# Small hashed shifts of the due times in a list-scheduled attention and two-layer feed-forward kernel

## The chip, the cores and the metric

The kernel runs on one NeuronCore of one Trainium2 chip. The metric is the time of one execution on the device, in microseconds (us): 919.58 is the median of three runs of the kernel before (918.4, 919.58, 921.48).

## What is computed

Windowed causal attention, then two feed-forward layers on its output, all in float32 with an error that a single low-precision pass doesn't reach:

```python
scores = q @ k.T / sqrt(64) + alibi bias            # 4 batches, 8 heads, 576 positions, window 128
attn = exp(scores - max) / (sum + 1e-9)
x = (attn @ v)                                      # 2304 tokens x 512
g = x @ w_gate; x = (g * sigmoid(g)) * (x @ w_val) @ w_out1     # inner width 1536
h = x @ w_in;   out = (h * sigmoid(h)) @ w_out2                 # inner width 2048
```

## The kernel before, in words

The 2304 tokens are 18 tiles of 128, worked through in three parts of six tiles. Each part runs the first layer (`moe1`) and the second (`moe2`); the attention of the next part runs between their products. Every float32 operand is split into a high and a low half (`copy_op` or L353 makes the high one, `sum_op` or L362/L363 the low one), and each product is three matmuls: high by high, high by low, low by high (`passes`, L932 to L934; `out1`, L1296 to L1298; `late_out2`, L1217 to L1219; `out2`, L1329 to L1331). The wide products go by a Strassen-like scheme (`quad`): seven products instead of eight on sums of operands and weights, in three PSUM banks X, Y and Z. Between them ACT copies a bank to SBUF (`copy` in `quad`, L353 into `tmp`) and DVE adds a copy to a bank (L979, L994). `operands` (L713, L353, L362) makes the sums and halves of the inputs at the start of each layer. Attention has its own lines: transposes L450 and L458, scores L498, masks L525, bias and maximum L532, exponent L538, the inverse of the row sum L554 and L555, scaling L558 on POOL, a transpose L575, a copy to `u` (L353), two triangular selections L582 and L589, the product with v L612 and its halves L353 and L653. Weights are loaded (L771), turned into words (L772 on ACT into `top`, L775 on DVE into `word`), split, kept in DRAM and fetched again by the parts that follow (L792, L921).

No order of work is written out. Each piece is given to `Plan.add` with an engine, a cost in ns, a due time in ns and the keys that it reads and writes. `Plan.issue` then plays the engines against the clock of its costs: again and again it takes, over all engines, the piece that can start first; where several on an engine are ready, the one with the earliest due time goes first (`insort(ready[e], (ops[n][1], n))`). Pieces that can run on two engines (`copy_op`: ACT or DVE; `sum_op`: POOL or DVE) go to the one that is expected to end sooner. What comes out is one fixed instruction order for each engine and for SP's queue of DMAs; on the chip every engine takes its instructions in that order and waits where an input isn't there yet. So a due time decides two things only: who goes first among the ready, and with it which engine a piece lands on.

Of the kernel before, what the change touches and what calls it, by code (L numbers as in the profile page):

```python
# [20 lines left out]
P = 128  # L21
BIG = 1.0e9
HUGE = 3.0e38


COST = {
# [30 lines left out]
class Plan:  # L57
# [19 lines left out]
    def add(self, engine, cost, due, fn, reads=(), writes=(), take=None, give=None, port=False, other=(), slack=0.0):  # L77
        n = len(self.ops)
        preds = set()
        for key in reads:  # L80
            if key in self.writer:
                preds.add(self.writer[key])
            self.readers.setdefault(key, []).append(n)
        for key in writes:
            if key in self.writer:
                preds.add(self.writer[key])
            preds.update(self.readers.pop(key, ()))
            self.writer[key] = n
        preds.discard(n)
        if isinstance(take, Bank):  # L90
            take = (take,)
        ways = {e: (c, f, p or e == "pool", d) for e, c, f, p, d in [(engine, cost, fn, port, 0.0), *other]}
        self.ops.append((ways, due, preds, take, give, slack))

    def issue(self):
        ops = self.ops
# [107 lines left out]
def attention_moe_moe2_kernel(  # L204
# [303 lines left out]
    def attend(i, hf, dues, banks):  # L508
# [7 lines left out]
        def scores(e, due):  # L516
# [12 lines left out]
            def biased():  # L529
                for p in range(2):  # L530
                    l = 2 * p + e
                    nc.vector.tensor_tensor_reduce(  # L532
                        t[:, l, :], cur()[:, p, :], alibi[:, 4 * hf + l, :], 1.0, HUGE, ALU.add, ALU.min, st[:, 0, l:l + 1]
                    )
# [272 lines left out]
    def strassen_sums(a, due, slack=0.0):  # L807
        def add(x, y, op):
            i = take("sum", len(SUM_R))
            t, tk = SUM_R[i], ("sum", i)  # L810
            (xa, xk), (ya, yk) = x, y
            sum_op(2 * P, due, lambda: t, lambda: xa, lambda: ya, op, xk + yk, [tk], slack=slack)
            return t, [tk]

        s1 = add(a[1, 0], a[1, 1], ALU.add)
        s2 = add(s1, a[0, 0], ALU.subtract)
        s3 = add(a[0, 0], a[1, 0], ALU.subtract)
        s4 = add(a[0, 1], s2, ALU.subtract)
        return s1, s2, s3, s4
# [732 lines left out]
```

## Time and profile before

| | |
|---|---|
| median of three runs | 919.58 us (918.4 to 921.48) |
| the profiled execution | 919.92 us; its span, first to last instruction, 918.2 us |
| TensorE matmul (PE) busy | 899.8 us, 98% of the span, 5938 matmuls |
| VectorE (DVE) busy | 724.0 us, 79% |
| GpSimd (POOL) busy | 605.5 us, 66% |
| ScalarE (ACT) busy | 556.5 us, 61% |
| chain that ended last | PE 76%, DVE 12%, ACT 4%, POOL 4%, DMA 3%, issue 2% |

Busy PE is not PE at its peak: matmuls are pipelined, the end of each is modelled, and two in a row overlap. A wait therefore shows smaller as idle time than it costs. The distance between the starts of two matmuls is the honest measure.

### The profile page before, as it was taken

The page shows a single profiled execution, that of the slowest core. Times are in us where ns is not written, and L with a number is a line of the kernel's source. Part 1 is how long each engine was busy: PE and PEld are TensorE (multiplying, and loading weights), DVE is VectorE, ACT ScalarE, POOL GpSimd, SP SyncE. Part 2 cuts the span into 40 slices and gives each one's busy share as a digit, 9 for nine tenths or more (in the row PEclk, how much of TensorE's full clock was granted, in tenths as well). Part 3 has the DMA queues.
Part 4 walks back from the last instruction along what each step waited for, and adds up shares of the span by engine and source line. Part 5 has one row for each costly group of instructions (what it writes and reads, how often), then busy time and mean ns, then how long its engine had stood idle before and what let it go on. Part 6 is the DMA issues. An engine that isn't in the chain of part 4 may idle for free.

```text
span 918.2 us, 18574 instructions
## 1 busy us (share of the span) xinstructions
PE 899.8 (98%) x5938; PEld 850.3 (93%) x5938; DVE 724.0 (79%) x1687; ACT 556.5 (61%) x1431; POOL 605.5 (66%) x697
## 2 busy tenths in 40 slices
PE   8999999999999999999999999999999999999998
PEld 7888999999888888999999899999799999999997
DVE  8898978989899898879888989897736666836664
ACT  6877666767867775865555586664463333484531
POOL 3756657875767588996566787686444446697564
PEclk9999999999999999999999999999999999999999
DMA  9998878896687977998878577679788788578702
GB/s 224 283 290 253 288 260 289 285 301 218 227 278 239 290 267 260 316 335 277 267 237 287 160 255 266 226 266 342 269 270 254 250 249 252 184 247 251 233 1 92
DMA packets 179233, 230.34 MB, mean 251 GB/s; under 512 B 68160, under 2 KB 90432, under 8 KB 179136
## 3 DMA queue, kind: packets, MB, share of 16 engines
q1 hardware_dynamic: 179136, 229.17, 77.7%
q8 instruction: 47, 0.77, 0.4%
q14 instruction: 50, 0.41, 0.1%
HBM read 152.31 MB, written 76.81 MB: 250 GB/s over the span
## 4 chain that ended last, share of the span: by engine, by line
PE 76%; DVE 12%; ACT 4%; POOL 4%; DMA 3%; issue 2%; SPq 0%; DVEq 0%; POOLq 0%; ACTq 0%
PE bank L932 16%; PE bank L933 15%; PE bank L934 15%; PE bank L612 3%; PE bank L1217 3%; PE bank L1219 3%; PE bank L1218 3%; PE bank L1329 3%; PE bank L498 3%; PE bank L1331 3%; PE bank L1330 3%; PE bank L1296 2%; PE bank L1297 2%; PE bank L1298 2%; POOL ACC L363 2%
## 5 line engine op out<-in xcount | busy, mean ns | idle before, releaser
L932 PE MATMUL bank<-XOP,wu 128*128 128x384 f32 (+1 forms) x868 | 297.2, 342 | 6.7 <-ACT tmp L353 4.9
L933 PE MATMUL bank<-XOP,wu 128*128 128x384 f32 (+1 forms) x868 | 288.8, 333 | 2.1 <-DVE XOP L362 1.3
L934 PE MATMUL bank<-XOP,wu 128*128 128x384 f32 (+1 forms) x868 | 288.6, 332 | 0.0
L932 PEld LDWEIGHTS bank<-XOP,wu 128*128 128x128 f32 x868 | 163.0, 188 | 18.0 <-ACT tmp L353 9.5
L933 PEld LDWEIGHTS bank<-XOP,wu 128*128 128x128 f32 x868 | 163.3, 188 | 3.6 <-DVE XOP L362 2.1
L934 PEld LDWEIGHTS bank<-XOP,wu 128*128 128x128 f32 x868 | 163.0, 188 | 0.0
L353 ACT ACTIVATE tmp<-bank 128x384 f32<-128x384 f32 x139 | 65.1, 489 | 60.5 <-PE bank L934 38.5
L363 POOL TENSOR_TENSOR h<-tmp,h 128x384 fp32r<-128x384 f32 x67 | 68.3, 1028 | 36.9 <-ACT h L353 36.4
L1194 DVE TENSOR_TENSOR ACC<-bank,ACC 128x384 f32<-128x384 f32 (+2 forms) x144 | 74.4, 551 | 3.9 <-PE bank L934 1.6
L363 POOL TENSOR_TENSOR wu<-word,wu 128x256 fp32r<-128x256 f32 x60 | 51.5, 864 | 34.9 <-ACT wu L353 14.5
L558 POOL TENSOR_TENSOR cs<-cs,st 128x512 f32<-128x512 f32 x36 | 39.4, 1093 | 51.3 <-DVE st L555 17.1
L979 DVE TENSOR_TENSOR bank<-bank,tmp 128x384 f32<-128x384 f32 x93 | 51.9, 559 | 21.0 <-PE bank L934 16.1
L772 ACT ACTIVATE top<-raw 128x512 f16<-128x512 bf16 x68 | 54.2, 797 | 20.7 <-DVE word L775 16.3
L1194 DVE TENSOR_TENSOR XST<-bank,XST 128x512 f32<-128x512 f32 (+1 forms) x108 | 57.3, 553 | 11.8 <-PE bank L1219 6.0
L363 POOL TENSOR_TENSOR wu<-sums,wu 128x256 fp32r<-128x256 f32 x79 | 63.1, 824 | 4.3 <-ACT wu L353 2.3
L775 DVE SCALAR_TENSOR_TENSOR word<-raw,top 128x512 int32<-128x512 int32 x68 | 56.6, 833 | 7.2 <-ACT top L772 6.3
L353 ACT ACTIVATE h<-tmp 128x384 fp32r<-128x384 f32 x75 | 38.9, 522 | 37.0 <-DVE tmp L1067 12.3
L538 ACT ACTIVATE cs<-cs,st 128x128 f32<-128x128 f32 x144 | 56.1, 394 | 7.9 <-DVE st L532 7.7
L1329 PE MATMUL bank<-wo,h 128*128 128x512 f32 (+1 forms) x146 | 58.5, 401 | 0.3 <-DVE XOP L362 0.3
L363 POOL TENSOR_TENSOR wo<-word,wo 128x256 fp32r<-128x256 f32 (+1 forms) x34 | 32.8, 967 | 39.2 <-ACT wo L353 31.9
L1331 PE MATMUL bank<-wo,h 128*128 128x512 f32 (+1 forms) x146 | 57.4, 393 | 0.0
L1330 PE MATMUL bank<-wo,h 128*128 128x512 f32 (+1 forms) x146 | 57.4, 393 | 0.0
(400 smaller groups left out, 2478.3 us busy)
## 6 DMA issues: line engine op xcount, KB each, us to landing
wu<-kept_i SPq DMA_DIRECT2D x112, 256.0 KB, 3.1
wu<-kept_g SPq DMA_DIRECT2D x72, 256.0 KB, 3.5
wu<-kept_v SPq DMA_DIRECT2D x72, 256.0 KB, 3.2
kept_s<-wo SPq DMA_DIRECT2D x66, 256.0 KB, 2.7
raw<-in_moe_w_out_dram SPq DMA_DIRECT2D x28, 512.0 KB, 5.3
kept_i<-wu SPq DMA_DIRECT2D x56, 256.0 KB, 4.6
kept_g<-wu SPq DMA_DIRECT2D x42, 256.0 KB, 5.3
kept_v<-wu SPq DMA_DIRECT2D x42, 256.0 KB, 5.4
```

What stands on the lines that cost most here:

```text
L353: act = lambda: nc.scalar.activation(out(), src(), AF.Copy)
L363: pool = lambda: nc.gpsimd.tensor_tensor(out(), x(), y(), op)
L538: nc.scalar.activation(t[:, l, :], t[:, l, :], AF.Exp, bias=st[:, 0, l:l + 1], scale=-1.0, accum_out=st[:, 1, l:l + 1])
L772: plan.add("act", 650.0, due, lambda: nc.scalar.activation(top16, bits, AF.Copy), [rk], [tk])
L775: lambda: nc.vector.scalar_tensor_tensor(w.bitcast(I32), word, 13, top, ALU.logical_shift_right, ALU.bitwise_or),
L932: nc.tensor.matmul(ps, wh, xh, start=start, stop=False, skip_group_check=True)
L933: nc.tensor.matmul(ps, wh, xl, start=False, stop=False, skip_group_check=True)
L934: nc.tensor.matmul(ps, wl, xh, start=False, stop=stop, skip_group_check=True)
L1194: plan.add("dve", cost("dve", n), due, lambda: nc.vector.tensor_tensor(acc, pv(), acc, ALU.add), [b], keys, give=b)
L1329: nc.tensor.matmul(ps, hh, wh, start=(i == 0), stop=False)
L1330: nc.tensor.matmul(ps, hh, wl, start=False, stop=False)
L1331: nc.tensor.matmul(ps, hl, wh, start=False, stop=(i == 1))
```

## The change

Each due time under `BIG` gets a shift that depends on the number of the piece and on a seed; the seed is looked up in a table by the 10 us stretch of planned time that the due time lies in. Seed 0 leaves the stretch alone. 34 of the 88 stretches have another seed: the shift then lies between -599 and +599 ns. 2532 of the 5759 pieces get one. The ten blank lines after `handover` make room, so that every line after it stands 13 lower in the new file.

```diff
+ORDER = (
+    1, 0, 0, 7, 2, 6, 0, 0, 0, 0, 8, 0, 0, 0, 0, 12, 0, 0, 0, 0, 0, 0, 0, 0, 0, 0, 10, 0, 15, 5, 0, 0, 0,
...
+)
+
+
+def shifted(due, n):
+
+    w = int(max(due, 0.0) // 10000)
+    seed = ORDER[w] if w < len(ORDER) else 0
+    return due + (((n + 1) * (2 * seed + 1) * 40503 >> 3) % 1024 - 511.5) * 1.1719 if seed and due < BIG else due
...
-        self.ops.append((ways, due, preds, take, give, slack))
+        self.ops.append((ways, shifted(due, n), preds, take, give, slack))
```

Over the whole program no instruction is added or removed, but some change engine: 26 pieces go from DVE to POOL, 17 from POOL to DVE, 22 from ACT to DVE and 16 from DVE to ACT. On PE 1396 of 1638 pieces keep their order among themselves, on SP's queue 681 of 804 (and no transfer moves more than nine places). Three places show what it does.

ACT at the start of the program, around the copy of the transposed weights of the second head half to `u` (`u_124`), which L612 on PE multiplies with v. Before:

```order
L538 ACTIVATE cs,st_121<-cs,st_121 128x128 x2
L353 ACTIVATE wu_73<-word_95 128x256
L461 ACTIVATE qts<-bank_130 128x256
L353 ACTIVATE wu_74<-word_95 128x256
L772 ACTIVATE top_94<-raw_92 128x512
L353 ACTIVATE u_124<-bank_131 128x512
L538 ACTIVATE cs,st_122<-cs,st_122 128x128 x2
```

With the change:

```order
L474 ACTIVATE qts<-bank_132 128x256
L785 ACTIVATE top_94<-raw_91 128x512
L366 ACTIVATE KR<-bank_129 128x2x128
L366 ACTIVATE u_124<-bank_135 128x512
L366 ACTIVATE u_123<-bank_130 128x512
L474 ACTIVATE qts<-bank_131 128x256
```

The copy to `u_124` has moved up past two weight halves (`wu`) and the conversion of a second weight tile (`top_94<-raw_92`).

DVE at 505 to 511 us, around the low halves of two hidden blocks (`h_105`, `h_102`) that L1297 on PE waits for. Before:

```order
L1067 SCALAR_TENSOR_TENSOR tmp_108<-tmp_108,tmp_113 128x384
L979 TENSOR_TENSOR bank_130<-bank_130,tmp_111 128x384
L1067 SCALAR_TENSOR_TENSOR bank_130<-tmp_107,bank_130 128x384
L554 TENSOR_SCALAR st_121<-st_121 128x4
L555 RECIPROCAL st_121<-st_121 128x4
L1067 SCALAR_TENSOR_TENSOR bank_135<-tmp_109,bank_135 128x384
L362 TENSOR_TENSOR h_105<-bank_130,h_105 128x384
L362 TENSOR_TENSOR later_top_256_148<-word_98,later_top_256_148 128x256
L362 TENSOR_TENSOR h_102<-bank_135,h_102 128x384
```

With the change:

```order
L992 TENSOR_TENSOR bank_135<-bank_135,tmp_111 128x384
L1080 SCALAR_TENSOR_TENSOR bank_135<-tmp_107,bank_135 128x384
L477 SCALAR_TENSOR_TENSOR qts<-bank_128,qts 128x256
L375 TENSOR_TENSOR h_105<-bank_135,h_105 128x384
L1080 SCALAR_TENSOR_TENSOR bank_129<-tmp_109,bank_129 128x384
L1080 SCALAR_TENSOR_TENSOR tmp_108<-tmp_108,tmp_113 128x384
L375 TENSOR_TENSOR h_102<-bank_129,h_102 128x384
L567 TENSOR_SCALAR st_121<-st_121 128x4
L568 RECIPROCAL st_121<-st_121 128x4
```

The product into `tmp_108`, the inverse of the row sum (L554 and L555, now L567 and L568) and a product into a bank have moved from ahead of `h_105` to behind it; the low half of a query tile (`qts`) has come in front.

PE at 661 us, at the start of the first layer of the last part: the second product of the blocks in `bank_134` and `bank_132` (weights `wu_81`, `wu_82`), whose inputs `operands` has just made. Before:

```order
L932 MATMUL bank_135<-XOP,wu_87 128x384
L933 MATMUL bank_135<-XOP,wu_87 128x384
L934 MATMUL bank_135<-XOP,wu_87 128x384
L932 MATMUL bank_134<-XOP,wu_81 128x384
L933 MATMUL bank_134<-XOP,wu_81 128x384
L934 MATMUL bank_134<-XOP,wu_81 128x384
L932 MATMUL bank_132<-XOP,wu_82 128x384
```

With the change:

```order
L945 MATMUL bank_134<-XOP,wu_87 128x384
L946 MATMUL bank_134<-XOP,wu_87 128x384
L947 MATMUL bank_134<-XOP,wu_87 128x384
L945 MATMUL bank_131<-XOP,wu_73 128x384
L946 MATMUL bank_131<-XOP,wu_73 128x384
L947 MATMUL bank_131<-XOP,wu_73 128x384
L945 MATMUL bank_133<-XOP,wu_74 128x384
L946 MATMUL bank_133<-XOP,wu_74 128x384
L947 MATMUL bank_133<-XOP,wu_74 128x384
L945 MATMUL bank_130<-XOP,wu_81 128x384
```

Two products (`wu_73`, `wu_74`, three matmuls each) of the other weight stand ahead of `wu_81` now; they followed it before.

## Rows read from the trace of the kernel before

**Rows 1.** The page, part 1: busy time of each engine.
```profile
PE 899.8 (98%) x5938; PEld 850.3 (93%) x5938; DVE 724.0 (79%) x1687; ACT 556.5 (61%) x1431; POOL 605.5 (66%) x697
```
**Rows 2.** Waits of PE, the largest of 14 kinds: us in all, times, longest.
```profile
PE bank L932 <- ACT tmp L353: 4.9, 7, 1.2
```
**Rows 3.** Busy time by stretch: length; PE, PEld, DVE, ACT, POOL; clock, DMA share, GB/s.
```profile
0.00:100.00 100.00, 94.20 (x823) 84.60 (x824) 88.56 (x313) 75.88 (x244) 55.65 (x70) 1.00 0.94 267
180.00:200.00 20.00, 20.00 (x117) 19.97 (x117) 16.42 (x31) 12.49 (x27) 16.14 (x19) 1.00 0.98 329
```
**Rows 4.** Timeline, 402 to 427 us: start, length, engine; in brackets idle time before, releaser.
```profile
405.27 0.34 PE L934 MATMUL bank<-later_raw,wo 128*128 128x384 f32 x1
...
406.28 0.45 PE L932 MATMUL bank<-XOP,wu 128*128 128x384 f32 x1 [0.67 <-ACT tmp L353]
...
406.68 0.49 ACT L353 ACTIVATE later_raw<-bank 128x384 fp32r<-128x384 f32 x1 [0.45 <-DVE bank L1123]
...
425.44 0.45 PE L932 MATMUL bank<-XOP,wu 128*128 128x384 f32 x1 [0.33 <-ACT tmp L353]
```
**Rows 5.** Timeline, 17 to 20 us, ACT and PE.
```profile
17.93 0.78 ACT L772 ACTIVATE top<-raw 128x512 f16<-128x512 bf16 x1
18.56 0.57 ACT L353 ACTIVATE u<-bank 128x512 f32<-128x512 f32 x1
...
19.19 0.66 PE L612 MATMUL bank<-u,vld 128*64 128x128 f32 x8 [1.07 <-ACT u L353]
```
**Rows 6.** Timeline, 44 to 87 us, PE alone.
```profile
45.02 0.39 PE L932 MATMUL bank<-XOP,wu 128*128 128x256 f32 x1 [0.79 <-DVE XOP L653]
...
82.97 0.44 PE L932 MATMUL bank<-XOP,wu 128*128 128x384 f32 x1 [0.41 <-DVE h L362]
...
86.49 0.39 PE L933 MATMUL bank<-XOP,wu 128*128 128x256 f32 x1 [0.84 <-DVE XOP L653]
```
**Rows 7.** Timeline, 505 to 534 us, DVE and PE.
```profile
505.61 1.22 DVE L1067 SCALAR_TENSOR_TENSOR tmp<-tmp,tmp 128x384 f32<-128x384 f32 x1
...
509.87 0.44 PE L1297 MATMUL bank<-h,wo 128*128 128x384 f32 x1 [0.91 <-DVE h L362]
...
511.43 0.45 PE L1297 MATMUL bank<-h,wo 128*128 128x384 f32 x1 [0.23 <-DVE h L362]
...
519.44 0.45 PE L933 MATMUL bank<-XOP,wu 128*128 128x384 f32 x1 [0.61 <-DVE XOP L362]
...
533.26 0.44 PE L932 MATMUL bank<-XOP,wu 128*128 128x384 f32 x1 [1.24 <-ACT tmp L353]
```
**Rows 8.** Timeline, 657 to 666 us, PE alone.
```profile
657.35 0.44 PE L933 MATMUL bank<-XOP,wu 128*128 128x384 f32 x1 [0.26 <-DVE XOP L362]
...
659.19 0.44 PE L932 MATMUL bank<-XOP,wu 128*128 128x384 f32 x1 [0.70 <-ACT tmp L353]
...
662.40 0.44 PE L933 MATMUL bank<-XOP,wu 128*128 128x384 f32 x1 [0.43 <-DVE XOP L362]
...
665.23 0.44 PE L932 MATMUL bank<-XOP,wu 128*128 128x384 f32 x1 [0.63 <-ACT tmp L353]
```
**Rows 9.** Timeline, 609 to 795 us, PE alone: two more waits.
```profile
609.88 0.39 PE L1217 MATMUL bank<-wo,h 128*128 128x256 f32 x1 [0.83 <-DVE later_raw L362]
...
794.87 0.45 PE L932 MATMUL bank<-XOP,wu 128*128 128x384 f32 x1 [1.13 <-ACT tmp L353]
```
**Rows 10.** Groups on DVE by form: count, busy us, mean ns; idle before, releasers.
```profile
L1067 DVE SCALAR_TENSOR_TENSOR tmp<-tmp,bank 128x384 f32<-128x384 f32 x57 | 31.2, 547 | 12.1 <-PE bank L934 8.8 <-ACT tmp L1056 2.6
...
L1067 DVE SCALAR_TENSOR_TENSOR tmp<-tmp,tmp 128x384 f32<-128x384 f32 x37 | 26.2, 709 | 0.8 <-ACT tmp L1056 0.6
```
**Rows 11.** Timeline, 625 to 630 us: two halves of an output weight on DVE and POOL.
```profile
625.02 0.68 DVE L362 TENSOR_TENSOR wo<-word,wo 128x512 fp32r<-128x512 f32 x1
...
628.65 1.30 POOL L363 TENSOR_TENSOR wo<-word,wo 128x512 fp32r<-128x512 f32 x1 [5.12 <-PE bank L1219]
```
**Rows 12.** The page, part 6: DMA issues, KB each, us from issue to landing.
```profile
wu<-kept_i SPq DMA_DIRECT2D x112, 256.0 KB, 3.1
```

2 rows, old and new, of the table ORDER are left out of this document.

## The prediction

> **What bounds the kernel now.** I read the page first: the matmul row says 899.8 us of 918.2 [rows 1]. Taken as it stands that leaves 18.4 us of idle time, and every other engine is far from full. Then the waits of PE [rows 2], to see who ends its idle time: the largest kind is a product that waits for ACT's copy of a bank to `tmp`, 4.9 us in seven places; no kind among the 14 names a transfer. Then the timeline at each place. One of them [rows 4] shows how a wait is to be read: the matmuls at 405.27 and 406.28 us start 1.01 us apart; in a dense stretch 117 matmuls take 20.00 us, 0.17 each [rows 3]. So this wait costs 0.84 us where the bracket says 0.67. The rest is the overlap of two matmuls. I add 0.17 to every bracket from here on.
>
> The places that I can name are these, with what each costs by that rule. Start-up: 1.24 at 19.19 us [rows 5]; 0.96, 0.58 and 1.01 at 45.02, 82.97 and 86.49 us [rows 6]. Middle: 0.84 and 0.50 at 406.28 and 425.44 us [rows 4]; 1.08, 0.40, 0.78 and 1.41 from 509.87 to 533.26 us [rows 7]. Start of the last part: 0.43, 0.87, 0.60 and 0.80 from 657.35 to 665.23 us [rows 8]. Two more: 1.00 and 1.30 at 609.88 and 794.87 us [rows 9]. Together 13.8 us in 16 places. All else PE does back to back at the full clock, 1.00 in both stretches of [rows 3]. A change of order alone can win at most about this, and can lose without such a bound, since any matmul can be put ahead of its input.
>
> **The change, part by part.** It adds no work, so each term is a wait that shrinks, grows or appears. A wait shrinks by what PE now does ahead of the waiting product, and by what the engine waited for now does after it instead of before; it grows the other way.
>
> *Start-up.* At 19.19 us L612 waits for ACT's copy of `u`, which ends at 19.13, behind a conversion of 0.78 us for a weight tile that nobody needs yet [rows 5]. In the new order the copy stands ahead of that conversion and of two weight halves. Its transposes are still needed first, so I leave a third of the wait and take 0.9 off. At 45.02 us a product waits for the low half of the second tile pair's attention result (L653). That instruction stands 15 places lower on DVE now. DVE is 88.56 us busy in the first 100, by 313 instructions [rows 3], 0.28 each; some that now stand ahead are the dearer ones, so I put 5.3 us on the 15 places, the upper end, and 4.2 is the lower. On PE the waiting product also stands lower, behind 46 matmuls more: 5.2 us at the stretch's mean of 0.114 (94.20 by 823), some 4.0 if these, transposes and scores in the main, are shorter. Net between 1.0 less and 1.3 more; I take 1.3 more, since DVE is nearly full there. At 82.97 us the waiting product stands behind 52 matmuls more and its latest input only five places lower on DVE: the 0.58 goes. At 86.49 us input and product both move up four pieces, DVE's ahead being the longer: 0.6 off. In all 0.8 us less. Bounds: 2.8 less (the other three gone, the one at 45.02 unchanged) and 5.3 more (DVE's 15 places uncovered).
>
> *Middle, 400 to 430 us.* At 406.28 us three products of 3 x 0.17 us and four transposes now stand ahead of the waiting product, some 1.9 us. But ACT's queue has three instructions more ahead of the copy, 0.5 us each, and one of them is the copy to `later_raw` that itself waited for DVE until 406.68 us [rows 4]. I take 0.3 off; the bounds are 0.84 less and 0.6 more. At 425.44 us one product more stands ahead, 0.52 us against a cost of 0.50: 0.5 off. In all 0.8 less.
>
> *505 to 534 us.* The low half of `h` that PE waits for at 509.87 us had a DVE instruction of 1.22 us [rows 7] ahead of it, and the inverse of a row sum; both now stand behind. That is more than the 1.08, even though PE itself comes 0.5 us earlier: gone, and the 0.40 at 511.43 with it, as its input follows. At 519.44 us four products more stand ahead, 2.1 us, against two or three DVE instructions more, up to 1.6 by 0.55 each [rows 10]: the 0.78 goes. At 533.26 us three products of `late_out2` and `quad` come in, 1.6 us, and transposes of 0.5 go out: 1.07 of 1.41 off. In all 3.3 less; with none of it the bound is 0.
>
> *657 to 666 us.* The first two waits keep their order on PE, ACT and DVE to the instruction: 0. At 662.40 us two products more stand ahead, 1.04 us: 0.60 off. At 665.23 us five more, 2.6 us: 0.80 off. In all 1.4 less.
>
> *609.88 and 794.87 us.* PE's pieces, and those right ahead on the engine waited for, stand as before: 0.
>
> *Engines changed.* The clearest is a half of an output weight at 625.02 us that goes from DVE, 0.68 us, to POOL, 1.30 us. POOL had been idle 5.12 us before 628.65 us [rows 11], and this covers it. Were it not covered, the sums that follow on POOL would start 1.30 us later, and with them the last part.
>
> *SP's queue.* No transfer moves more than nine places and none of PE's waits names one: 0. Without that cover a load costs one landing, 3.1 us [rows 12], at its place.
>
> *New waits.* 242 pieces on PE leave their old order, and the trace of before can't show what waits they meet. I put three new ones of 0.40 us, the size of the smallest named wait but one: 1.2 us more. Bounds: 0, and the whole 6.3 us of the savings.
>
> Sum: 0.8 + 0.8 + 3.3 + 1.4 - 1.2 = 5.1 us less, against the profiled execution's own 919.92 us: **914.8 us**. The profiled execution lies 0.3 us above the median; I leave that, as a difference of 0.3%, 2.8 us, is about what a measurement of this kernel can tell from none.
>
> **Rivals.** *The waits come back one instruction later.* In start-up and from 505 to 534 us DVE sets the pace; a product that no longer waits may only bring PE sooner to the next thing DVE is late with. For it: 88.56 of 100 us busy [rows 3]. Against it: over the whole span DVE is 79% busy [rows 1]. Then only 425.44, 662.40 and 665.23 us hold, 1.9 less, and 1.2 new: 919.2 us.
>
> *Everything that moved is won.* All 13.8 but the four places that keep their order (1.00, 1.30, 0.43, 0.87), and nothing new: 10.2 less, 909.7 us. Against it: the product at 45.02 us, whose input sinks by more than it does.
>
> *DVE and POOL get in each other's way.* A product with both inputs in SBUF takes 709 ns on the mean, the same with one input in PSUM 547 [rows 10]; single ones take 1.22 us [rows 7], 0.67 over the 547, while POOL works. The new order sends 26 pieces from DVE to POOL, 17 back, and shifts hundreds of others against each other, so more of the instructions that PE waits for can meet a POOL instruction. At 0.67 a meeting, 14 of them in waited-for places are 9.4 us: 914.8 + 9.4 = 924.2. It decides from 11 on (914.8 + 7.5 passes 922.3). Against it: the place at 509.87 us, where such an instruction has left the path. The Trainium skill, SBUF — State Buffer, section Who interferes with whom, says that a VectorE instruction with two SBUF inputs and a GpSimd instruction that reads SBUF exclude each other for a whole instruction. This speaks against a change that reshuffles the two; the 709 against 547 ns agree with it, and no row here shows how many meetings the new order makes.
>
> *The change does nothing.* The three pieces of order above rule that out.
>
> **How the numbers follow.** The forecast has 0.47, waits that come back 0.25, everything won 0.12, DVE and POOL 0.16. Around 914.8 I allow 911.5 to 918.5: the give-back from 0 to 3.7 us more. Faster by over 0.3% (below 916.8): 0.41 of the forecast's 0.47 and the 0.12, 0.53. Within 0.3%: its other 0.06 and 0.21 of the waits that come back, 0.27. Slower (above 922.3): 0.04 of those and the 0.16, 0.20. The range is 909 to 922.5: it leaves out half of everything won, and most of DVE and POOL, under 0.2 together.
>
> **What the new profile would show.** Right: the brackets at about 510, 519 and 533 us, and the two at 662 and 665, gone or under 0.3, those at 610 and 795 as they were, the one at 45 us larger. The matmul row's idle time near 14 us. Wrong: as many brackets as before, at other instructions of the same producers (waits that come back); the mean of `tmp<-tmp,tmp` above 0.8 us (DVE and POOL); a wait of PE that names a transfer (the queue); or start-up longer by more than 2 us, which would mean that the 15 places on DVE count in full.

## The result and the profile after

The changed kernel takes **910.75 us** (median of five runs, 909.84 to 911.17) against 919.58. The ratio to runs of before on the same chip is 0.9901, with a 95% interval of 0.9886 to 0.9916: 8.8 us less, where 5.1 less was forecast and the range began at 909. The profiled execution took 909.84 us. Its page has these rows, which answer to [rows 1]:

```profile
span 908.2 us, 18541 instructions
...
PE 894.3 (98%) x5938; PEld 849.4 (94%) x5938; DVE 718.4 (79%) x1684; ACT 556.6 (61%) x1425; POOL 612.1 (67%) x706
```

The matmuls leave 13.9 us idle (908.2 less 894.3) where they left 18.4. The waits of PE (columns: who waits for whom, us in all, times, longest) answer to [rows 2]:

```profile
PE bank L945 <- ACT tmp L366: 2.7, 3, 1.1
PE bank L1309 <- DVE st L545: 1.5, 1, 1.5
...
PE bank L588 <- POOL cs L571: 1.2, 2, 0.8
PE bank L945 <- ACT XOP L366: 0.8, 1, 0.8
PE bank L463 <- DMA klds<-in_k_dram: 0.7, 1, 0.7
```

The wait for ACT's copy to `tmp` fell from 4.9 us in seven places to 2.7 in three. Of its eleven kinds seven are new; the four largest of these are shown, one of them a transfer. The timeline of PE shows where they lie (a line L stands 13 lower than before):

```profile
18.45 0.66 PE L463 MATMUL bank<-ident,klds 128*128 128x128 f32 x4 [0.65 <-DMA klds<-in_k_dram]
...
45.92 0.38 PE L1309 MATMUL bank<-h,wo 128*128 128x256 f32 x1 [1.47 <-DVE st L545]
...
404.13 0.33 PE L947 MATMUL bank<-later_raw,wo 128*128 128x384 f32 x1
404.30 0.34 PE L945 MATMUL bank<-XOP,wu 128*128 128x384 f32 x1
...
513.58 0.41 PE L945 MATMUL bank<-XOP,wu 128*128 128x384 f32 x1 [0.85 <-ACT XOP L366]
521.03 0.44 PE L946 MATMUL bank<-XOP,wu 128*128 128x384 f32 x1 [0.24 <-DVE XOP L375]
527.69 0.44 PE L945 MATMUL bank<-XOP,wu 128*128 128x384 f32 x1 [0.55 <-ACT tmp L366]
...
602.01 0.28 PE L1230 MATMUL bank<-wo,h 128*128 128x256 f32 x1
...
651.59 0.44 PE L945 MATMUL bank<-XOP,wu 128*128 128x384 f32 x1 [1.03 <-ACT tmp L366]
785.22 0.44 PE L945 MATMUL bank<-XOP,wu 128*128 128x384 f32 x1 [1.14 <-ACT tmp L366]
```

Between 120 and 430 us no bracket is left: the product that started at 406.28 us [rows 4] starts at 404.30, 0.17 behind its neighbour. The brackets from 509.87 to 519.44 [rows 7] are gone, but 513.58 and 521.03 are new. The one at 609.88 [rows 9] is gone: that product starts at 602.01, with none. Those at 662 and 665 us [rows 8] are gone; 659.19 stands, at 651.59 and with 1.03 where it had 0.70, and 794.87 [rows 9] stands at 785.22.

To see where the time went I read a **lead**: how much earlier than in the profiled execution of before the same matmul starts, at points where both kernels have done the same matmuls. An example outside such points shows the reading: 609.88 less 602.01 is 7.87. The table has the leads at seven points of before's time, for the change and for each kernel of the next section (us; more is earlier). All are differences between single executions.

| kernel | 165 | 350 | 431 | 495 | 591 | 628 | 670 | end |
|---|---|---|---|---|---|---|---|---|
| the change | 2.3 | 2.4 | 4.9 | 5.0 | 6.8 | 8.0 | 9.4 | 10.1 |
| e13_again, the same once more | 2.4 | 2.4 | 4.9 | 5.0 | 6.9 | 8.0 | 9.4 | 10.1 |
| e1_start | 1.4 | 1.1 | 1.0 | 1.1 | 1.0 | 1.1 | 1.3 | 1.5 |
| e2_middle | 1.2 | 0.8 | 3.1 | 3.3 | 4.6 | 4.7 | 5.0 | 5.2 |
| e3_late | 0.6 | -0.4 | -0.5 | -0.5 | 0.1 | 1.2 | 2.1 | 2.6 |
| e10_mid1 | 0.7 | 0.6 | 2.8 | 2.8 | 2.8 | 2.8 | 3.4 | 3.6 |
| e11_mid2 | 1.8 | 0.8 | 0.8 | 0.5 | 1.9 | 1.6 | 1.1 | 1.3 |
| e5_order | -0.4 | -1.4 | -0.6 | -0.6 | 1.6 | 2.7 | 0.5 | 0.1 |
| e9_slack | 0.5 | 0.6 | 3.0 | 3.2 | 5.1 | 6.2 | 7.8 | 8.4 |
| e12_pinmid | 2.4 | 2.6 | 5.0 | 5.1 | 6.4 | 7.5 | 9.2 | 9.9 |
| e4_other | -0.2 | -1.3 | 0.5 | 0.5 | 0.0 | 0.9 | 0.8 | 0.7 |
| e6_other2 | -5.6 | -6.7 | -8.3 | -8.4 | -7.0 | -6.1 | -4.8 | -5.4 |
| e7_engines | -2.5 | -2.6 | -1.0 | -0.9 | -1.6 | -1.6 | -2.8 | -3.5 |

The change gains at five places and keeps each gain: 2.3 us in start-up, 2.5 from 350 to 431, 1.8 from 495 to 591, 1.1 at 610, 1.5 from 628 to 670; 0.6 more comes in small steps from there to the end. The table of seeds has 91 entries, where the text on the change speaks of 88 stretches.

The first gain needs care: 0.9 of the 2.3 us is there at 6.66 us, up to which both kernels do the same matmuls in the same order. Here is PE, first before and then with the change:

```profile
4.83 0.63 PE L1379 MATMUL bank<-bigt 128*128 128x128 f32 x2
5.25 0.63 PE L458 MATMUL bank<-ident,qlds 128*128 128x128 f32 x2
```
```profile
4.75 0.39 PE L1392 MATMUL bank<-bigt 128*128 128x128 f32 x2
4.97 0.38 PE L471 MATMUL bank<-ident,qlds 128*128 128x128 f32 x2
```

The first pairs of matmuls start 0.43 us apart and later ones 0.22; the closer spacing begins at about 6.5 us in the execution of before and at about 4.4 in that of the change. The clock column gives 1.00 for both stretches, so the profile doesn't say why. At 8.5 us, still in one order, the other four executions that begin as before does (e2, e3, e10, e11) lead by 0, 0.9, 0 and 1.1: this part is chance.

### The profile page after: what moved, and what is told of

Read it like the earlier page. It is cut to its first block, busy times and chain, and to the rows that moved or that the text cites. A ratio compares the mean times of both kernels' runs of the same rounds, so it can differ in the third digit from the quotient of the medians.

```text
span 908.2 us, 18541 instructions
## 1 busy us (share of the span) xinstructions
PE 894.3 (98%) x5938; PEld 849.4 (94%) x5938; DVE 718.4 (79%) x1684; ACT 556.6 (61%) x1425; POOL 612.1 (67%) x706
## 4 chain that ended last, share of the span: by engine, by line
PE 77%; DVE 12%; POOL 4%; ACT 3%; DMA 2%; issue 2%; SPq 0%; DVEq 0%; ACTq 0%; POOLq 0%
PE bank L945 16%; PE bank L946 16%; PE bank L947 16%; PE bank L1230 3%; PE bank L1232 3%; PE bank L1231 3%; PE bank L625 3%; PE bank L1342 3%; PE bank L1343 2%; PE bank L1344 2%; PE bank L511 2%; PE bank L1310 2%; POOL ACC L376 2%; PE bank L1309 2%; PE bank L1311 2%
## 5 line engine op out<-in xcount | busy, mean ns | idle before, releaser
L1080 DVE SCALAR_TENSOR_TENSOR bank<-tmp,bank 128x384 f32<-128x384 f32 (+1 forms) x81 | 44.2, 547 | 12.1 <-ACT tmp L1069 7.4
```

## The experiments

Twelve kernels ran, each timed beside the kernel before, whose median was 919.97 us beside the first four, 919.64 beside the next four and 919.67 beside the last. The **theory** at the start: each stretch of the plan wins or loses its own waits. Its rivals: any shuffle does it; or not the order but the pieces that changed engine.

**One group of stretches alone.** Three kernels keep the seeds of one part of the table and set the rest to 0:

```diff
-    seed = ORDER[w] if w < len(ORDER) else 0
+    seed = ORDER[w] if w < 10 else 0          # e1_start: 4 seeds
+    seed = ORDER[w] if 10 <= w < 48 else 0    # e2_middle: 14 seeds
+    seed = ORDER[w] if 48 <= w < len(ORDER) else 0   # e3_late: 16 seeds
```

*e1_start.* 

> Seeds of the stretches up to 60 us of planned time alone (the first four), all others 0. Theory (gains are local and add up): the order on PE follows the changed kernel's up to about 165 us and the old kernel's from there; the trace of the changed kernel is 2.3 us ahead of the old one's at that point, so 2.3 us faster than before, about 917.3. Rival (one early shift carries through the whole plan, and the waits later on go because of it): more than 4 us faster. Rival (start-up is set by VectorE, which the order can't relieve): within 1 us of before.

Measured: 919.42 us, ratio 0.9999 (0.9990 to 1.0008). The profiled execution led by 1.4 us, the median of eleven runs by nothing.

*e2_middle.* 

> Seeds of the stretches from 100 to 470 us of planned time alone (fourteen of them). Theory (local): the lead that the changed kernel gains between 165 and 562 us of the trace, 6.9 - 2.3 = 4.6 us; about 915. Rival (the early shift matters for these): under 2 us faster.

Measured: 914.67 us, ratio 0.9947 (0.9935 to 0.9960).

*e3_late.* 

> Seeds of the stretches from 480 us of planned time on alone (sixteen). Theory (local): the lead gained after 562 us of the trace, 10.0 - 6.9 = 3.1 us, among it the wait at 610 us and the two at 662 and 665 us; about 916.5. Rival (the waits at 610 and 660 us went because of shifts upstream): under 1 us faster, and these waits still there. The three kernels together should give the whole, 8.8 us by the medians, if gains add.

Measured: 917.04 us, ratio 0.9973 (0.9962 to 0.9984).

By the ratios the three give 0.1, 4.9 and 2.5 us, together 7.5 of the change's 9.1; the 1.6 between them lie inside the intervals. The table shows the gains of e2_middle between 350 and 591 us and those of e3_late between 591 and 670, where the change has them. So the seeds act where they stand. Start-up didn't give the 2.3 us of its lead, and repeats say why. Leave out the first 8.5 us, in which all have one order, and read what each gains from there to 112 us. The five profiled executions with before's order (before itself, e2, e3, e10, e11) gain 0, 0.7, -0.2, 0.7 and 0.7, on the mean 0.4. Of the five with the change's order four (the change, e13, e12, e1) gain 1.0, 1.0, 1.1 and 0.9; the fifth, e9_slack, a variant of the change that comes below, loses 0.5. Here are PE and a stretch of the clock in e9_slack (columns as in [rows 3]; lines 16 below those of before), and the same stretch in the change:

```profile
46.33 0.58 PE L1312 MATMUL bank<-h,wo 128*128 128x256 f32 x1 [1.45 <-DVE st L548]
47.00:49.00 2.00, 2.00 (x11) 1.96 (x10) 1.68 (x10) 1.22 (x5) 0.00 (x0) 0.50 1.20 257
```
```profile
47.00:49.00 2.00, 2.00 (x25) 1.69 (x23) 1.91 (x9) 1.71 (x7) 0.38 (x1) 1.00 1.16 298
```

Both have the same wait, 1.45 us here and 1.47 in the change. Behind it the granted clock of e9_slack falls to 0.50, the lower of TensorE's two levels (1.2 and 2.4 GHz), from 46.3 to 49.7 us, and e9_slack falls 1.45 us behind the change by 112 us; the change stays at 1.00. So the order is worth some 0.6 us in start-up (1.0 less 0.4) where the clock holds, and this wait can cost more than that where it doesn't.

**Other seeds in the same stretches.**

```diff
-    seed = ORDER[w] if w < len(ORDER) else 0
+    seed = (ORDER[w] + 6) % 15 + 1 if w < len(ORDER) and ORDER[w] else 0    # e4_other
+    seed = (ORDER[w] + 2) % 15 + 1 if w < len(ORDER) and ORDER[w] else 0    # e6_other2
```

*e4_other.* 

> The same 34 stretches, each with another seed (6 on, around from 15 to 1). Theory (it matters which waits an order happens to open or close, so the seed does the work): the old waits that cost 14 us are traded for new ones of like size, within 4 us of before, 916 to 924. Rival (any disturbance of the old order helps, since the old one was a poor one): 5 to 9 us faster, 911 to 915.

Measured: 919.91 us, ratio 1.0002 (0.9994 to 1.0011).

*e6_other2.* 

> The same stretches as the change with a second set of other seeds; 200 pieces on PE move. Theory (a shuffle as such is worth nothing on the mean; these seeds were picked): 918 to 922. Rival (the first other set was an unlucky one): 915 or less.

Measured: 925.52 us, ratio 1.0063 (1.0046 to 1.0079). It loses 5.6 us before 165 us and 2.8 more up to 495, and wins back some from there on. The timeline of PE in e6_other2 shows the largest of its waits; the second row is a stretch behind it with the granted clock, 0.50 (columns as in [rows 3]):

```profile
84.70 0.44 PE L625 MATMUL bank<-u,vld 128*64 128x128 f32 x4 [2.74 <-DVE tmp L1080]
88.00:92.00 4.00, 4.00 (x20) 4.00 (x19) 2.02 (x5) 2.04 (x5) 1.90 (x3) 0.50 0.77 224
```

The clock stands at 0.50 from 85.8 to 92.6 us. Of the 5.6 us the wait takes 2.8, and 2.4 more go by 112 us, the stretch at 0.50 among them; all six runs of this kernel list a mean clock below 1 (0.996 to 0.998).

A shuffle as such didn't help: one set gives no difference, one costs 5.8 us, the chosen one wins 9. The choice of seeds does it.

**Order or engines?** The change moves 81 pieces to another engine. e5_order takes its due times and holds these pieces on the engines of before; e7_engines takes the due times of before and holds them where the change has them:

```diff
+        if n in PIN:
+            ways = {PIN[n]: ways[PIN[n]]}
```

*e5_order.* 

> The changed dues as they are, but the 81 pieces that change their engine with them are held on the engines they had before; the order on PE stays nearly that of the change (245 pieces moved against 242). Theory (the gain comes from the order in which PE takes its work against the producers' order): within 1.5 us of the change, 909.5 to 912.5. Rival (it is the pieces that went from DVE to POOL and back that relieve the waits): half of the gain or more is lost, 914 or more.

Measured: 921.39 us, ratio 1.0019 (1.0009 to 1.0028).

*e7_engines.* 

> The dues of before, with the 81 pieces held on the engines that the change gives them; 115 pieces on PE move in consequence. Theory (order, not engines): no gain that can be measured, 918 to 922. Rival (the engines): half of the gain or more, 915.5 or less.

Measured: 919.94 us, ratio 1.0011 (1.0002 to 1.0021).

Both simple answers fall: neither half wins anything alone. The leads of e5_order tell more. It wins 2.2 us from 495 to 591 and 1.1 at 610, as the change does, and loses 1.0 before 350 and 2.2 from 628 to 670. The timelines of PE and ACT in e5_order (lines 28 below those of before; the last row is a stretch, with its clock) name what it meets:

```profile
36.80 0.39 PE L960 MATMUL bank<-XOP,wu 128*128 128x256 f32 x1 [1.15 <-DVE wu L382]
...
340.32 0.45 PE L960 MATMUL bank<-XOP,wu 128*128 128x384 f32 x1 [0.87 <-DVE tmp L1022]
...
655.39 1.76 ACT L381 ACTIVATE XOP<-XST 128x384 fp32r<-128x384 f32 x4 [1.49 <-DMA XST<-kept_x]
655.97 0.44 PE L960 MATMUL bank<-XOP,wu 128*128 128x384 f32 x1 [2.78 <-ACT XOP L381]
658.00:660.00 2.00, 2.00 (x8) 1.74 (x8) 2.00 (x6) 1.36 (x4) 2.00 (x2) 0.50 1.04 416
```

At 655.97 us PE stands for 2.78 us behind ACT, and ACT behind a transfer that is late; why it is late no row here shows. Behind the wait the clock stands at 0.50 from 657.2 to 660.6 us (the last row), and the lead falls by 1.9 more. All ten runs of e5_order list a mean clock of 0.994 to 0.998. So the order's own gains in the middle are there, and new waits, with the lower clock behind the longest, eat them: that e5_order comes out at 921.39 doesn't show that an order is worth nothing without its engines. e7_engines has such stretches in its profiled execution too, the slowest of its twelve (50.3 to 53.8 and 661.3 to 664.7 us); its runs that list a clock of 1.00 lie at 919.6 to 920.5, so it wins nothing even so. Due times set order and engine in one go, and these seeds gain as a pair. A pure order can't be had in this planner: holding the 81 lets 31 other pieces change engine.

**Half of the middle.**

```diff
+    seed = ORDER[w] if 26 <= w < 40 else 0    # e10_mid1
+    seed = ORDER[w] if 40 <= w < 47 else 0    # e11_mid2
```

*e10_mid1.* 

> The seeds of the stretches from 260 to 400 us of the plan alone. Theory (each wait is won or lost where its stretch is; between 355 and 430 us the change gained 0.7 and 1.8): 1.8 to 2.7 less than before, 917.2 to 918.2, and the trace in front of 350 us and behind 440 as before. Rival (the gain of the middle is one chain, of which the first part alone gives nothing): 919 to 920.5.

Measured: 916.25 us, ratio 0.9967 (0.9955 to 0.9979), 3.0 us less.

*e11_mid2.* 

> The seeds of the stretches from 400 to 470 us of the plan alone. Theory (local; the change gained 1.6 between 495 and 537 us): 1.4 to 2.0 less than before, 917.6 to 918.4, the lead coming between 500 and 575 us. The forecast's own term for that place was 3.3, which would give 916.4. Rival (it needs the stretches in front): 919 to 920.5.

Measured: 917.82 us, ratio 0.9981 (0.9972 to 0.9989), 1.8 us less.

The two give 4.8 us together where e2_middle gave 4.9. In the table e10_mid1 wins 2.2 between 350 and 431 us and nothing on to 628; e11_mid2 wins 1.4 between 495 and 591. Local gains add up.

e10_mid1 gains a little more than its place shows. A likely reason stands on DVE at 337 us, where before's order has three sums of weights behind a load. Here are DVE in before, and DVE and PE in e3_late, whose order is the same up to there:

```profile
336.85 0.43 DVE L362 TENSOR_TENSOR sums<-word,word 128x256 f32<-128x256 f32 x1 [0.77 <-DMA word<-kept_wg]
```
```profile
336.56 1.10 DVE L375 TENSOR_TENSOR sums<-word,word 128x256 f32<-128x256 f32 x1 [1.02 <-DMA word<-kept_wg]
...
339.34 0.44 PE L945 MATMUL bank<-XOP,wu 128*128 128x384 f32 x1 [0.87 <-DVE tmp L1007]
```

The same sum takes 0.43 us in one execution and 1.10 in the other, POOL being at work in both; where it takes 1.10, PE waits 0.87. Two of four profiled executions with this order paid that wait (e3_late, e11_mid2; not before and e1_start). e5_order, which holds the sums on DVE too, has the same 0.87, but not from this: its sum takes 0.42, and two others right behind it on DVE take 1.12 and 1.24. The seeds of e10_mid1 send the three sums to POOL. At 1.04 us (0.87 and the 0.17) in half the executions that is an estimated 0.5 us that the profile of before couldn't show.

**Two tries to beat the change.** e9_slack counts two conversions of operands on ACT as ready 1.5 us later in the plan, so that at the two largest brackets left ACT copies to `tmp` first:

```diff
+SLACK = {4387: 1500.0, 5103: 1500.0}
...
-        self.ops.append((ways, shifted(due, n), preds, take, give, slack))
+        self.ops.append((ways, shifted(due, n), preds, take, give, slack + SLACK.get(n, 0.0)))
```

*e9_slack.* 

> The change, and in two places (the largest brackets left in the second half, 1.03 us at 651.59 and 1.14 us at 785.22) ACT's copy of a bank to tmp goes ahead of the copy that itself waits for DVE. Theory (ACT's order alone makes these two waits): both brackets fall under 0.4, 1 to 2 us less than the change, about 909. Rival (the product then waits for the next thing that is late there): same as the change, 910.5 to 911.

Measured: 911.69 us, ratio 0.9911 (0.9898 to 0.9924). Both brackets fell; the timelines of ACT and PE in e9_slack show what came:

```profile
651.51 0.49 ACT L369 ACTIVATE tmp<-bank 128x384 f32<-128x384 f32 x1 [0.32 <-PE bank L950]
...
653.09 1.28 ACT L1062 ACT_TABLE_LOAD   x1
654.38 0.49 ACT L1062 ACTIVATE vld<-bank 128x384 f32<-128x384 f32 x1
```
```profile
654.92 0.44 PE L948 MATMUL bank<-XOP,wu 128*128 128x384 f32 x1 [0.34 <-ACT vld L1062]
...
655.79 0.44 PE L948 MATMUL bank<-XOP,wu 128*128 128x384 f32 x1
...
786.34 0.44 PE L948 MATMUL bank<-XOP,wu 128*128 128x384 f32 x1 [0.58 <-ACT tmp L369]
```

The 1.03 at 651.59 became 0.34 at 654.92, behind a table load of 1.28 us on ACT, and 0.24 more at 655.79 (0.41 from the start before it, at 655.38, where 0.17 is usual). The 1.14 became 0.58. The lead grows by 1.6 from 628 to 670, against the change's 1.5. Here the rival holds that I had given a quarter: the waits come back one instruction later. That the median lies a microsecond above the change's is another matter: the two runs at 912.25 (the profiled one, with its clock at 0.50 in start-up) and 912.61 list a mean clock of 0.998, the two at 910.49 and 911.13 one of 1.000 and 0.999.

e12_pinmid is the change with nine pieces between 477 and 521 us held on the engines of before, where e5_order had done better than the change:

```diff
+PIN = {
+    3453: "act", 3467: "dve", 3622: "dve", 3654: "act", 3656: "dve",
+    3660: "act", 3662: "dve", 3678: "dve", 3697: "dve",
+}
```

*e12_pinmid.* 

> The change with nine pieces between 477 and 521 us held on the engines of before (five on DVE instead of ACT or POOL, four the other way or back); from 480 to 545 us its order is that of the kernel that held all 81, which showed one bracket of 0.55 there where the change has 1.64 in three. Theory (a wait is won where its own stretch is rearranged, whatever the rest does): 0.5 to 1.0 us less than the change in the same call, and the brackets at about 514 and 528 gone. Rival (the pieces take the gain back later): same as the change within 0.3.

Measured: 911.33 us, ratio 0.9915 (0.9902 to 0.9928), beside 910.35 for the change, measured along with it. Its timeline of PE:

```profile
513.53 0.44 PE L954 MATMUL bank<-XOP,wu 128*128 128x384 f32 x1 [0.55 <-DVE XOP L383]
522.23 0.39 PE L1238 MATMUL bank<-wo,h 128*128 128x256 f32 x1 [0.98 <-DVE XOP L383]
```

The bracket at 514 us is smaller, the one at 528 is gone, and 0.98 at 522.23 is new: no gain, 1.3 us of lead from 495 to 591 where the change has 1.8. Here the nine pieces behave as a part of the whole; what a held stretch did in one surrounding it doesn't do in another.

**The change again.** *e13_again.* 

> The changed kernel once more, as the measure beside which the next three stand on the same chip in the same call. Theory (the gain holds from one profile to the next, but start-up varies by a microsecond or two with the order unchanged): 910 to 912, the lead over before from 165 us to the end 7.5 to 7.9 again, the lead at 165 us somewhere between 0.5 and 2.4. Rival (the 9 us were partly a lucky series): 913 or more.

Measured: 910.35 us, ratio 0.9903 (0.9891 to 0.9916). Its leads agree with those of the first profile to 0.1 us at every point. Nothing that ran beats it.

## Why the prediction was right

The direction and the mechanism hold, waits of PE that close one by one; of 8.8 us, 5.1 were forecast. That the time lies in the range says little: of the twelve kernels above only one, e6_other2, lies outside 909 to 922.5. The profile leads by 10.1 us, 5.0 more than forecast: 1.5 of these are in start-up, 0.9 of that chance; 1.7 from 350 to 431; 1.1 at 610; 0.6 behind 670, where the forecast had nothing. Term by term, by the leads:

*Start-up, 0.8 less.* From 8.5 to 112 us 1.0 less, of which executions in before's own order gain 0.4 on the mean; e1_start's median shows nothing, and its interval allows 0.9 less to 0.7 more. It isn't settled closer. In parts: to 26 us 0.35 less where 0.9 was forecast, since 19.19 went but 18.45 and a wait of 0.82 for POOL's `cs` came; from there to 79 us 1.1 more, where 1.3 more was forecast; from there to 112 us 1.7 less, where 1.2 was. The step on 45.02 us was about right in its sum for a wrong reason: no wait for the attention result (`XOP`, L653, now L666) is listed any more, but a product of another line waits in its place, 1.47 at 45.92, for the bias and maximum of a row (`st`, L532 before, L545 now) on DVE. That is no input of a product of `h` and `wo`: as at 610 us, below, what is given back there is a bank, and in the plan it is the bank that this product takes.

*400 to 430 us, 0.8 less.* Mis-sized: 2.5 less from 350 to 431, and e10_mid1 alone shows 2.2. I kept 0.54 of the wait at 406.28 for three more instructions on ACT; but the copy to `later_raw` among them no longer waits for DVE, and the row at 404.30 has nothing left. ACT in the changed kernel:

```profile
402.12 0.49 ACT L366 ACTIVATE later_raw<-bank 128x384 fp32r<-128x384 f32 x1
```

And I left out 356 us, where the kernel before has a bracket of 0.34 (0.51 by my own rule) and some smaller ones follow that have no name. It isn't the only one: "all else back to back" was wrong by six brackets of the kernel before, 0.66, 0.28, 0.28, 0.34, 0.17 and 0.16 at 21.53, 22.20, 60.69, 356.00, 483.35 and 578.48 us, 2.9 us by the rule.

*505 to 534 us, 3.3 less.* Mis-sized the other way: 1.8 less from 495 to 591, 1.6 of it by 537. What was to go went: 509.87, 511.43 and 519.44, 2.26 together. At 533.26 there are 0.72 left (0.55 and 0.17) where 0.34 should be. And two new brackets, 0.85 and 0.24, cost 1.4 by the same rule: 1.5 less in all. This is where the term *new waits*, 1.2 more, lies; with it the forecast was 2.1. A third new one, 0.45 at 566.81, costs 0.6 that is won back by 579 us.

*657 to 666 us, 1.4 less.* 1.5 from 628 to 670. The two waits that were to go went; of the two that were to stay, 657.35 has 0.18 left and 659.19 grew to 1.03.

*609.88 us, 0.* **This step failed**: 1.1 less, with e3_late alone as well. I had looked at PE's neighbours and at the pieces right ahead on the engine waited for. The row of before names DVE's `later_raw<-bank,later_raw`. That isn't an input of a product of `wo` and `h`; what it gives back is a bank. In the new order this shows on DVE in the changed kernel:

```profile
602.80 0.56 DVE L375 TENSOR_TENSOR later_raw<-bank,later_raw 128x384 fp32r<-128x384 f32 x1
```

It ends at 603.36, and the product starts at 602.01, before it: it has another bank. In the plan it takes the bank that this DVE piece gives back before, and with the change one that a copy on ACT gives back. Banks are handed out in the order in which pieces on PE take them, and six pieces further up one product of `late_out2` now goes ahead of two of `quad` and four transposes. In e2_middle, which lacks that swap, the bracket stands:

```profile
605.27 0.38 PE L1230 MATMUL bank<-wo,h 128*128 128x256 f32 x1 [0.83 <-DVE later_raw L375]
```

*794.87 us, 0.* Right: 1.13 became 1.14.

*The rivals.* Everything won would have been 909.7 and came closest in time, but not in kind: 1.4 us of new waits and 45.92 speak against it, and 610 us was no part of it. DVE and POOL fell, by the row that answers to [rows 10]:

```profile
L1080 DVE SCALAR_TENSOR_TENSOR tmp<-tmp,tmp 128x384 f32<-128x384 f32 x37 | 25.7, 695 | 1.6 <-ACT tmp L1069 1.3
```

695 ns where it was 709. Still e6_other2 landed near that rival's 924.2, with 707 ns in this row: a change of this kind can be that much slower, but by a wait in start-up and the lower clock behind it. In that rival's sum eleven meetings of 0.67 are 7.4 us, not 7.5, and reach 922.2: twelve are needed. Of the signs that I had named, a transfer that PE waits for did come, 0.65 at 18.45 us, and cost nothing that can be told from the spread of start-up.

## What to carry to other kernels

In a kernel that PE fills to 98%, what a new order is worth is the sum over the places where PE stands still, each read from its own stretch; here such gains added up when they were made apart. For each wait, ask whether it is for an input or for a bank: who holds a bank is decided by pieces well above the place. Don't expect half of a planner's gain from its order or its engines alone, or more of it by holding some pieces: here neither half won anything, as each met waits of its own. And look at the granted clock behind every long wait before you price it.

## What the runs showed of the hardware

With the order unchanged, one execution differs from the next by more than many changes are worth: 1.1 us in the first 7 us and 0.9 more by 112 us, 1 us at 340 us, where one sum on DVE takes 0.43 or 1.10 us. Here is POOL beside that sum, in e3_late (1.10 from 336.56 us) and in e1_start (0.43 from 335.74 us):

```profile
336.37 1.00 POOL L376 TENSOR_TENSOR XOP<-XST,XOP 128x384 fp32r<-128x384 f32 x1
```
```profile
335.75 1.29 POOL L376 TENSOR_TENSOR XOP<-XST,XOP 128x384 fp32r<-128x384 f32 x1
```

The Trainium skill, SBUF — State Buffer, section Who interferes with whom, says that a VectorE instruction with two SBUF inputs contends with a GpSimd instruction that reads SBUF, and that the order of issue decides who is held up. The rows agree: where POOL's instruction starts 0.19 us ahead of the sum, the sum is long; where it starts 0.01 us behind it, the sum is short and POOL's takes 1.29.

A long wait of PE can be followed by a lower clock, and then costs more than its length. The granted clock fell to 0.50 behind waits of 2.74 us (e6_other2), 2.78 (e5_order) and 1.45 (e9_slack), and came back to 1.00 while PE worked on. Behind the change's own 1.47 at 45.92 us it stayed at 1.00. So one profile doesn't show whether a place pays this.

The changed kernel's nine runs lie within 1.4 us (909.83 to 911.17), 22 runs of before within 3.8 (917.64 to 921.44). It may be that fewer places are left at which a late instruction reaches PE; no run here shows it.

A change of the function on ACT has a price of its own, 1.28 us for a table load, and in e9_slack it stands right ahead of the instruction that frees the bank PE waits for.
